# A linear-attention and spectral-mixing kernel on one core: batch 0 loaded in pieces with square-root norms, late transposes moved to transfers, and a new order of the work

## Chip, cores and metric

The kernel runs on one core of one Trainium2 chip. The metric is the device time of one launch in microseconds (us). Inputs and output lie in the chip's memory (HBM) as float32. The engines of the core are TensorE (PE for its matmuls, PEld for its weight loads), VectorE (DVE), ScalarE (ACT), GpSimd (POOL) and SyncE (SP). SP computes nothing here; it issues transfers. POOL also issues transfers, above all those that turn float32 into float16 on the way.

## What is computed

```python
# q, k, v: (8 batches, 8 heads, 576 tokens, 64);  D = C = 512 = 8 * 64
kv  = einsum('bhsd,bhse->bhde', k, v)
raw = einsum('bhsd,bhde->bhse', q, kv)
x   = raw / sqrt(mean(raw**2, -1) + 1e-6) * g_norm      # then heads side by side: (8, 576, 512)

theta = x @ w_theta
zr, zi = x * cos(theta), x * sin(theta)
y   = einsum('ts,bsd->btd', w_tok_r, zr) + einsum('ts,bsd->btd', w_tok_i, zi)
u   = x + y
out = u + maximum(u @ w_ch, 0)
```

## The kernel before

The 576 tokens of a batch are cut into five tiles: four full ones of 128 tokens (j = 0 to 3) and a tail of 64 (j = 4), which is folded, two half-widths one above the other, so that it fills 128 partitions with 256 columns. The eight batches go through the same stages. For one batch b these are, by the names of the tasks that the order is written in:

- **load k, load v, load q**: k and v come in as float32 on SP's queue (those of batch 0 in halves of two head pairs each, k on SP's queue and v on ACT's). q comes in as float16 on POOL's queue, which also brings `wth` (w_theta) and the two token weights `toki` and `tokr`. `wch` (w_ch) comes in as float32 into the buffer of z of batch 1 and is scaled into float16 by four tasks `wc`. A tiny transfer `hold s` on SP reads the token weight `toki`; everything behind it on SP's queue waits until that has landed.
- **kv** (matmuls, L272 for batch 0, L279 else) and **ko** (copy into the block-diagonal `kbd`).
- **qt, qo**: q turned by TensorE against the identity and copied out, for batches 0 and 1. From batch 2 on (`QD = 2`) a transfer does it instead, **qd**: a DMA transpose issued by SP.
- **raw** (q times kv, L338 and L347), **sq** (square, ACT), **ss** (sum per head, DVE), **rt** (power of -1/2, POOL, L376), **x** (DVE, L399): the norm. Code for a norm by square root (ACT, **sr**) and reciprocal (DVE, **rc**) is there, but its condition `b < 0` is never met.
- **xt, xo**: x turned by TensorE, 4 turns of 128 columns for a full tile and 2 for the tail, then copied out of PSUM with the scale g into `xT`.
- **th** (theta, L435 and L438), **pt** (ACT, L451), **ar** and **ab** (DVE, L457 and L465), **si** and **co** (sine and cosine, ACT, L473 and L480), **z** (DVE, L493). The tail's z goes into a buffer `zf`; four transfers **zv** on POOL's queue move its quarters into `zt`, where the tail's cosine and sine parts stand one above the other.
- **y** (token mixing, L516): `yH b c part` is half H of the tokens (256 or 320 columns), channel block c, in three parts of three matmuls. Part 0 needs z of tiles 0 and 1, part 1 that of tile 2, part 2 that of tile 3 and `zt`. **wt, wo** turn the token weights for it at the start, in nine groups. **um** (DVE, L521) makes u.
- **ut, uo**: u turned back by TensorE and copied out on ACT. **v** (u times w_ch), **fin** (DVE, L556: maximum with 0 and the sum), **st** (store, SP).

The order is written out by hand: `TURNS` lists the numbers of all tasks, `play` issues them in that order, and each engine works its own instructions strictly in the order in which they were issued. A letter behind a number puts a copy on another engine (A for ACT, D for DVE). `r16` and `r4` are idle matmuls that keep TensorE running at the start. So a task that waits holds everything that stands behind it on its engine or queue, whatever that needs. Buffers limit how far ahead a stage can run: 4 accumulators in PSUM (`acc`), 2 for turned tiles (`tr`), 2 for raw, 2 buffers of k and v, 3 of z.

## Time and profile before

| What | Value |
|---|---|
| runs of the kernel before | 222.97, 224.63, 227.66 us; median 224.63 |
| profiled execution, its own time | 224.09 us |
| its span, first to last instruction | 222.3 us |
| mean granted TensorE clock | 0.977 |
| read from HBM, written to HBM | 33.06 MB, 9.44 MB |

The span is shorter than the profiled execution's time by 1.8 us. An instruction in the profile is named by its line in the kernel, its engine, and the tiles that it writes and reads. A matmul row "x4" is four matmuls. Matmuls overlap in the array, so the step from one to the next, which the chain of waits shows, is shorter than the duration of one.

### The profile page before, as it was taken

To read this page: it belongs to the slowest core of one execution; us is meant where nothing else is said; L and a number is where in the kernel's file an instruction comes from. 1 tells how busy PE (TensorE), PEld (TensorE's weight loads), DVE (VectorE), ACT (ScalarE), POOL (GpSimd) and SP (SyncE) were. 2 spreads that over 40 slices of the span, in tenths; PEclk is the share of its full clock that TensorE was granted. 3 is DMA by queue.
4 is the path that set the end of the run, shared out by engine and by line. 5 is a ranking of instruction groups with operands and counts; after the bars stand their busy time and mean duration, and the time that the engine had idled before them with its cause. 6 is when DMAs were issued, how large, how long until landed. Compare 5 with 4: busy or idle time off the path is not lost.

```text
span 222.3 us, 5652 instructions
## 1 busy us (share of the span) xinstructions
PE 202.9 (91%) x2266; PEld 143.2 (64%) x2266; DVE 175.2 (79%) x358; ACT 131.6 (59%) x258; POOL 103.4 (47%) x112
## 2 busy tenths in 40 slices
PE   7397896958999999899999999999999999999992
PEld 2295555634777776676685777776676766676760
DVE  4028677849898798978999899799989889978552
ACT  2036257534685369765999559778564978565041
POOL 8208601599448376536765439380926034212000
PEclk9969799987999999999999999999999999999999
DMA  6999999998969999958999999399734004204324
GB/s 213 243 210 195 252 256 363 282 216 97 169 115 136 232 359 300 202 131 232 289 167 198 218 346 167 93 266 227 209 98 146 0 12 133 86 21 128 111 69 170
DMA packets 58731, 40.88 MB, mean 184 GB/s; under 512 B 28114, under 2 KB 52306, under 8 KB 58706
## 3 DMA queue, kind: packets, MB, share of 16 engines
q1 hardware_dynamic: 43474, 31.73, 55.6%
q0 software_dynamic: 14688, 7.62, 25.1%
q10 hardware_dynamic: 544, 1.18, 1.6%
q8 instruction: 18, 0.29, 0.5%
q14 instruction: 7, 0.06, 0.1%
HBM read 33.06 MB, written 9.44 MB: 191 GB/s over the span
## 4 chain that ended last, share of the span: by engine, by line
PE 64%; DMA 24%; POOL 4%; issue 2%; SPq 2%; DVE 2%; ACT 0%; POOLq 0%; DVEq 0%
PE y L516 30%; DMA vt<-in_v_dram 11%; PE v L435 9%; PE th L435 9%; DMA wn<-in_moe_w_tok_i_dram 7%; PE kv L279 5%; PE xps L296 3%; PE ups L296 3%; PE raw L338 2%; DMA zt<-zf 2%; DMA qe<-in_q_dram 2%; DMA out_dram<-ot 2%; PE th L438 2%; POOL rt L376 2%; SPq L194 1%
## 5 line engine op out<-in xcount | busy, mean ns | idle before, releaser
L376 POOL TENSOR_TENSOR rt<-ss,mhalf 128x8 f32<-128x8 f32 (+1 forms) x40 | 62.1, 1556 | 60.2 <-DVE ss L369 56.7
L516 PE MATMUL y<-wT,zm 128*128 128x320 f16 (+1 forms) x512 | 77.9, 287 | 0.7 <-DVE zm L493 0.7
L516 PEld LDWEIGHTS <-zm 128*128 128x128 f16 x512 | 47.8, 98 | 15.2 <-DVE zm L493 0.9
L521 DVE SCALAR_TENSOR_TENSOR wn<-y,gcol,xT 128x320 f16<-128x320 f32 (+1 forms) x64 | 32.0, 511 | 8.9 <-PE y L516 8.6
L435 PE MATMUL th<-wth,xT 128*128 128x512 f16 x128 | 33.6, 390 | 0.0
L451 ACT ACTIVATE pt<-th 128x512 f32<-128x512 f32 (+1 forms) x40 | 22.0, 553 | 17.5 <-PE th L435 16.2
L435 PE MATMUL v<-wch,wn 128*128 128x512 f16 x128 | 32.1, 379 | 0.0
L499 POOL DMA_DIRECT2D zt<-zf x32 | 17.6, 557 | 30.5 <-DVE zf L493 17.0
L480 ACT ACTIVATE sc<-arg,quarter 128x512 f16<-128x512 f32 (+1 forms) x40 | 26.8, 675 | 3.8 <-DVE arg L465 3.8
L542 ACT ACTIVATE us<-ups 128x512 f32<-128x512 f16 (+1 forms) x40 | 21.6, 551 | 12.3 <-PE ups L296 11.0
L556 DVE SCALAR_TENSOR_TENSOR ot<-v,us 128x512 f32<-128x512 f32 (+1 forms) x40 | 25.0, 632 | 4.3 <-ACT us L542 1.8
L457 DVE SCALAR_TENSOR_TENSOR arg<-pt,th 128x512 f32<-128x512 f32 (+1 forms) x40 | 24.8, 628 | 2.2 <-ACT pt L451 1.7
L473 ACT ACTIVATE sc<-arg 128x512 f16<-128x512 f32 (+1 forms) x40 | 23.1, 586 | 5.1 <-DVE arg L457 5.1
L369 DVE TENSOR_REDUCE ss<-sqb 128x8 f32<-128x520 f32 x32 | 22.0, 687 | 4.2 <-ACT sqb L360 4.1
L360 ACT ACTIVATE sqb<-raw 128x512 f32<-128x512 f32 x32 | 19.0, 595 | 10.0 <-PE raw L338 9.6
L399 DVE TENSOR_TENSOR x<-raw,rt 128x512 f16<-128x512 f32 x32 | 21.9, 684 | 3.7 <-POOL rt L376 3.7
L493 DVE TENSOR_TENSOR zm<-x,sc 128x1024 f16<-128x1024 f16 x32 | 21.7, 685 | 2.1 <-ACT sc L480 1.9
L279 PE MATMUL kv<-vt,kt 128*64 128x64 f32 x560 | 18.6, 223 | 3.1 <-DMA vt<-in_v_dram 3.1
L251 ACT ACTIVATE xT<-xps,gcol 128x512 f16<-128x512 f16 (+1 forms) x24 | 15.1, 632 | 10.1 <-PE xps L296 10.0
L279 PEld LDWEIGHTS kv<-vt,kt 128*64 128x64 f32 x560 | 17.5, 138 | 4.3 <-issue 1.9
L516 PE MATMUL y<-wT,zt 128*128 128x320 f16 (+1 forms) x64 | 18.8, 294 | 0.6 <-DMA zt<-zf 0.6
L435 PEld LDWEIGHTS <-xT 128*128 128x128 f16 x128 | 12.0, 101 | 10.2 <-issue 1.4
(73 smaller groups left out, 237.1 us busy)
## 6 DMA issues: line engine op xcount, KB each, us to landing
out_dram<-ot SPq DMA_DIRECT2D x32, 256.0 KB, 3.0
kt<-in_k_dram SPq DMA_DIRECT2D x7, 1024.0 KB, 7.5
vt<-in_v_dram SPq DMA_DIRECT2D x7, 1024.0 KB, 10.9
qh<-in_q_dram POOLq DMA_DIRECT2D x7, 512.0 KB, 10.2
kt<-in_k_dram SPq DMA_DIRECT2D x2, 576.0 KB, 4.8
vt<-in_v_dram ACTq DMA_DIRECT2D x2, 576.0 KB, 9.4
zm<-in_moe_w_ch_dram SPq DMA_DIRECT2D x1, 1024.0 KB, 11.5
zt<-zf POOLq DMA_DIRECT2D x32, 32.0 KB, 3.6
```

Source lines behind the costliest of these rows:

```text
L279: nc.tensor.matmul(t[i * D:(i + 1) * D, hp - lo, :], kt[b % NKV][:, 2 * hp + i, j, :], vt[b % NKV][:, 2 * hp + i, j, :], start=(j == 0), s ...
L369: nc.vector.reduce_sum(out=ss[:], in_=sq_sb.pop((b, j))[:], axis=AXX)
L376: nc.gpsimd.tensor_tensor(out=rt[:], in0=ss[:], in1=mhalf[:, 0:h], op=ALU.pow)
L399: nc.vector.tensor_tensor(out=x_pair[b, p][:, :, a * HC:(a + 1) * HC].rearrange("p t (h e) -> p h t e", e=D), in0=r[:].rearrange("p (h t e ...
L435: nc.tensor.matmul(t[:], lhs[:, kc, columns(j)], w[:, kc, :], start=first, stop=last)
L451: nc.scalar.activation(out=pt[:], in_=th_ps[b, j][:], func=AFT.Copy, bias=MAGIC)
L457: nc.vector.scalar_tensor_tensor(out=arg[:, 0, :], in0=pt_sb.pop((b, j))[:], scalar=MAGIC, in1=th_ps.pop((b, j))[:], op0=ALU.subtract, op1 ...
L473: nc.scalar.activation(out=sc[:, 0, :], in_=arg_sb[b, j][:, 0, :], func=AFT.Sin, bias=0.0, scale=-TURN * SHRINK,)
L480: nc.scalar.activation(out=sc_sb[b, j][:, 1, :], in_=arg_sb.pop((b, j))[:, 1, :], func=AFT.Sin, bias=quarter[:], scale=-TURN * SHRINK,)
L516: nc.tensor.matmul(t[:, 0:hi - lo], s, wT[:, w, lo:hi], start=n == 0, stop=n == len(z) - 1)
L521: nc.vector.scalar_tensor_tensor(out=uTb[b % NUT][:, c, lo:hi], in0=y_ps.pop((b, h, c))[:, 0:hi - lo], scalar=gcol[:, 0:1], in1=xTb[b % NX ...
L556: nc.vector.scalar_tensor_tensor(out=ot[:], in0=v_ps.pop((b, j))[:], scalar=0.0, in1=u_sb.pop((b, j))[:], op0=ALU.max, op1=ALU.add,)
```

## The change

- **Loads of batch 0.** k and v come in three pieces (head pairs 0 and 1, pair 2, pair 3), k and v in turn, all on SP's queue. `hold s` now reads the first piece of v instead of the token weight. Behind it stand, in this order, `wch`, k and v of batch 1, and k and v of batch 2; before, `wch` stood behind batch 1. On POOL's queue the token weight `toki` now stands ahead of `wth`, and q of batch 1 follows the token weights directly. All four `wc` go to POOL.
- **Norms of batch 0** by square root on ACT and reciprocal on DVE, instead of the power on POOL. The table of the square root is loaded at the start, that of the sine after the last square root (task `sn`).
- **Tail of z in batches 0 and 1** (`ZD = 2`): four multiplications on DVE write the quarters straight into `zt`, instead of one multiplication into `zf` and four transfers.
- **x of batches 5, 6 and 7** (`XD = 5`) is turned by DMA transposes on SP (tasks `xd`), two full tiles in one, the tail by itself. `xo` then reads SBUF instead of PSUM.
- **u of batches 5 and 6**, full tiles (`UD`), is turned by DMA transposes on SP (tasks `ud`, two buffers). For these `um` writes u in another layout, with one more instruction for the half that holds the tail; ACT takes the maximum with 0 out of PSUM (task `vo`), and `fin` adds the turned u to it.
- **fin** writes over one of its inputs; the buffers `us` and `ot` (three each) become one ring of five.
- **TURNS** is new throughout. The parts of it that matter are quoted by the names of the tasks in the prediction.

```diff
@@ play order: all of TURNS is replaced
@@ numbers
     QD = 2
+    XD = 5
+    UD = (5, 6)
+    ZD = 2
...
+    NUD = 2
+    NOT = 5
@@ x turned by transfers
+    def x_turn_dma(b, p):
+        if p < 2:
+            d = work.tile([P, 2 * NKC, P], FP16, tag="qD", bufs=4, name="xd")
+            src = x_pair[b, p][:].rearrange("p t c -> p (t c)")
+            tr_ps["x", b, 2 * p], tr_ps["x", b, 2 * p + 1] = d[:, 0:NKC, :], d[:, NKC:2 * NKC, :]
+        else:
+            d = work.tile([P, NKC // 2, P], FP16, tag="qTe", bufs=3, name="xd")
+            src, tr_ps["x", b, NJ] = x_sb[b, NJ], d[:]
+        nc.sync.dma_start_transpose(out=d[:], in_=src)
@@ z_make
+        if not full(j) and b < ZD:
+            for i in range(2):
+                for hh in range(2):
+                    at, to = slice(hh * TL, (hh + 1) * TL), slice((1 - i) * TL, (2 - i) * TL)
+                    nc.vector.tensor_tensor(
+                        out=zt[b % NZ][to, hh * HC:(hh + 1) * HC],
+                        in0=x[at, :], in1=sc[at, i, :], op=ALU.mult,
+                    )
+            return
@@ u_make
+        parts = [(uTb[b % NUT][:, c, lo:hi], lo, hi)]
+        if b in UD:
+            parts = [(u_units(b)[:, 2 * h:2 * h + 2, c * P:(c + 1) * P], lo, lo + 2 * P)]
+            if h:
+                parts.append((u_at(b, c, NJ), SM, S))
...
+    def u_turn_dma(b, j):
+        d = work.tile([P, NKC, P], FP16, tag="ud", bufs=NUD, name="ud")
+        nc.sync.dma_start_transpose(out=d[:], in_=u_units(b)[:, j, :])
+        u_sb[b, j] = d[:].rearrange("p n c -> p (n c)")
+
+    def positive(b, j):
+        d = work.tile([P, C], FP32, tag="us", bufs=NOT, name="vs")
+        nc.scalar.activation(out=d[:], in_=v_ps.pop((b, j))[:], func=AFT.Relu)
+        v_ps[b, j] = d
@@ finish
+        if full(j) and b in UD:
+            ot = v_ps.pop((b, j))
+            nc.vector.scalar_tensor_tensor(
+                out=ot[:], in0=u_sb.pop((b, j)), scalar=TURN, in1=ot[:], op0=ALU.mult, op1=ALU.add,
+            )
+        else:
+            ot = u_sb.pop((b, j))
...
@@ loads of batch 0
-    for a, (lo, hi) in enumerate(((0, NH2), (NH2, NHP))):
-        both = [add(f"load {x}0{'ab'[a]}", e, lambda e=eng, t=t, src=src, lo=lo, hi=hi: pairs_in(e, t[0], src, 0, lo, hi))
-                for x, e, eng, t, src in (("k", "SP", nc.sync, kt, k), ("v", "ACT", nc.scalar, vt, v))]
+    for a, (lo, hi) in enumerate(((0, NH2), (NH2, NH2 + 1), (NH2 + 1, NHP))):
+        both = [add(f"load {x}0{'abc'[a]}", "SP",
+                    lambda t=t, src=src, lo=lo, hi=hi: pairs_in(nc.sync, t[0], src, 0, lo, hi))
+                for x, t, src in (("k", kt, k), ("v", vt, v))]
...
-    add("hold s", "SP", lambda: hold_sync(wn[1][0:1, 0, 0:1]), got["tok", 0])
+    add("hold s", "SP", lambda: hold_sync(vt[0][0:1, 0, 0, 0:1]), [early])
@@ norms of batch 0
-            if b < 0:
+            if b == 0:
                 sr = add(f"sr {b} {j}", "ACT", lambda b=b, j=j: square_root(b, j), [ss])
                 rt = add(f"rc {b} {j}", "DVE", lambda b=b, j=j: reciprocal(b, j), [sr], [("rt" + w, 4)])
@@ start
-        table(AFT.Sin)
+        table(AFT.Sqrt)
```

More of the change, by code (lines that the diff above doesn't have):

```diff
@@ L173 @@
     gate = const.tile([1, 1], FP32, name="gate")
-    gate_s = const.tile([1, 1], FP16, name="gate_s")
+    gate_s = const.tile([1, 1], FP32, name="gate_s")
     def full(j):
@@ L434, in dense @@
             if full(j):
-                nc.tensor.matmul(t[:], lhs[:, kc, columns(j)], w[:, kc, :], start=first, stop=last)
+                nc.tensor.matmul(t[:], lhs(kc), w[:, kc, :], start=first, stop=last)
             else:
@@ L520, in u_make @@
         lo, hi = HALVES[h]
[L521 to L524 removed]
+        y = y_ps.pop((b, h, c))
+        parts = [(uTb[b % NUT][:, c, lo:hi], lo, hi)]
[3 more added lines that the diff above has]
+                parts.append((u_at(b, c, NJ), SM, S))
+        for dst, s0, s1 in parts:
+            y_in, x_in = y[:, s0 - lo:s1 - lo], xTb[b % NXT][:, c, s0:s1]
+            if s1 - s0 == 2 * P and b in UD:
+                y_in, x_in = (a.rearrange("p (j s) -> p j s", j=2) for a in (y_in, x_in))
+            nc.vector.scalar_tensor_tensor(
+                out=dst, in0=y_in, scalar=gcol[:, 0:1], in1=x_in, op0=ALU.mult, op1=ALU.add,
+            )
     def u_turn(b, j):
[L527 removed]
         if full(j):
[L529 removed]
+            turned("ups", lambda i: u_at(b, i, j), NKC, ("u", b, j))
             return
@@ L540, in u_out @@
         n, e = (NKC, "") if full(j) else (NKC // 2, "e")
-        d = work.tile([P, n * P], FP32, tag="us" + e, bufs=3, name="us")
+        d = work.tile([P, n * P], FP32, tag="us" + e, bufs=NOT, name="us")
         nc.scalar.activation(
```

141 lines of the change are left out of this document (88 added, 53 removed), and 42 rows, old and new, of the table TURNS.

## Prediction

> **What bounds the kernel now.** I read the page first, then the stretches before and after the point where batch 0's token mixing is done, then the chain of waits.
>
> ```profile
> span 222.3 us, 5652 instructions
> ...
> PE 202.9 (91%) x2266; PEld 143.2 (64%) x2266; DVE 175.2 (79%) x358; ACT 131.6 (59%) x258; POOL 103.4 (47%) x112
> ...
> PE   7397896958999999899999999999999999999992
> ...
> DVE  4028677849898798978999899799989889978552
> ...
> PEclk9969799987999999999999999999999999999999
> DMA  6999999998969999958999999399734004204324
> ```
> TensorE (PE) is busy nearly throughout from the eleventh slice on (a slice is 5.6 us), VectorE (DVE) is close behind it; in the first ten both have gaps, while the transfers run at nine tenths.
>
> ```profile
> 0.00:60.00 60.00, 46.54 (x523) 31.92 (x524) 36.97 (x86) 25.67 (x49) 32.14 (x41) 0.91 1.06 228
> 60.00:217.30 157.30, 155.71 (x1742) 111.21 (x1741) 137.15 (x272) 105.56 (x210) 71.29 (x71) 1.00 0.75 167
> ```
> The columns are busy time and, in brackets, instructions. Busy time of PE is modelled, so I count its work from steps in the chain of waits (start, length, what):
>
> ```profile
> 57.48 0.22 PE xps L296 x4
> ...
> 58.66 0.86 PE th L435 x4
> 59.52 0.33 PE y L516 x3
> ...
> 61.05 0.56 PE th L438 x8
> ...
> 61.61 2.33 PE kv L279 x80
> ...
> 101.18 0.25 PE raw L347 x8
> ...
> 143.56 0.41 PE y L516 x3
> ```
> One batch: y 4 x 3 x (0.33 + 0.41) = 8.9 us; theta 4 x 0.86 + 0.56 = 4.0, and the same for v; the turns of x and of u, 18 x 0.055 each, 2.0 together; kv 2.3; raw, four tiles like a turned tile and the tail, 1.1. That is 22.3, or 178.4 for eight. Batch 0's kv has 144 instructions instead of 80, 1.9 more; turning the token weights (45 turns) adds 2.5 and q of batches 0 and 1 adds 2.0: 185 us of work in a span of 222.3, so 37 are lost. The last part of batch 0's mixing starts at 59.52. By 59.9 PE has done 30.6: batch 0 without v and u (19.2), the 2.5 and 2.0, and of batch 1 kv, raw, four turned tiles and three thetas (6.9). So **29 of the 37 us are lost in the first 60**.
>
> ```profile
> 216.92 1.03 PE L435 MATMUL v<-wch,wn 128*128 128x512 f16 x4
> ...
> 218.30 0.69 DVE L556 SCALAR_TENSOR_TENSOR ot<-v,us 128x512 f32<-128x512 f32 x1 [0.65 <-DMA out_dram<-ot]
> ```
> The last four matmuls start at 216.92, done at 217.8. From 59.9 to there 154.3 us of work take 158, so the middle loses 3.6, and 4.5 follow behind the last matmul. Lost: head 29.3, middle 3.6, end 4.5.
>
> **The head, what it waits for now.**
>
> ```profile
> 5.09 15.70 DMA wn<-in_moe_w_tok_i_dram
> ...
> 46.81 4.10 DMA qe<-in_q_dram
> ```
> ```profile
> 10.05 3.11 PE L272 MATMUL kv<-vt,kt 64*64 64x64 f32 x72 [3.53 <-DMA vt<-in_v_dram]
> ...
> 13.10 1.04 PE L296 MATMUL qps<-ident,qh 128*128 128x128 f16 x8
> ...
> 15.54 0.62 PE L338 MATMUL raw<-kbd,qT 128*128 128x128 f16 x8
> ...
> 17.45 4.89 POOL L376 TENSOR_TENSOR rt<-ss,mhalf 128x8 f32<-128x8 f32 x3 [3.69 <-DVE ss L369]
> ...
> 20.81 0.72 SPq L238 DMA_DIRECT2D gate_s<-wn  x1
> ...
> 25.34 0.68 DVE L399 TENSOR_TENSOR x<-raw,rt 128x512 f16<-128x512 f32 x1
> ```
> ```profile
> 47.42 0.68 DVE L493 TENSOR_TENSOR zm<-x,sc 128x1024 f16<-128x1024 f16 x1
> ```
> Batch 0's first kv waits for v until 10.05, the turned q starts at 13.10, the norms pass one by one through POOL from 17.45, the last x of a full tile ends at 26.0, and z of tile 3 at 48.1. SP issues nothing behind `hold s` until toki is there (20.81). The 4.10 are a stall: PE stands at `qte 1 4` for q's tail of batch 1, issued too late.
>
> **The change in the head.** The prices on ACT and DVE, and the transfers:
>
> ```profile
> L480 ACT ACTIVATE sc<-arg,quarter 128x512 f16<-128x512 f32 x32 | 22.8, 717 | 3.1 <-DVE arg L465 3.1
> L369 DVE TENSOR_REDUCE ss<-sqb 128x8 f32<-128x520 f32 x32 | 22.0, 687 | 4.2 <-ACT sqb L360 4.1
> L399 DVE TENSOR_TENSOR x<-raw,rt 128x512 f16<-128x512 f32 x32 | 21.9, 684 | 3.7 <-POOL rt L376 3.7
> ...
> L473 ACT ACTIVATE sc<-arg 128x512 f16<-128x512 f32 x32 | 19.8, 629 | 2.8 <-DVE arg L457 2.7
> ...
> L451 ACT ACTIVATE pt<-th 128x512 f32<-128x512 f32 x32 | 19.0, 596 | 16.2 <-PE th L435 16.2
> ...
> L251 ACT ACTIVATE xT<-xps,gcol 128x512 f16<-128x512 f16 x18 | 12.2, 686 | 5.8 <-PE xps L296 5.7
> ...
> L301 ACT COPY wT<-wps 128x576 f16<-128x576 f16 x3 | 1.9, 633 | 4.9 <-PE wps L583 4.9
> ...
> L390 ACT ACT_TABLE_LOAD x1 | 1.3, 1283 | 0.7 <-PEq L806 0.7
> ```
> ```profile
> kt<-in_k_dram SPq DMA_DIRECT2D x2, 576.0 KB, 4.8
> ...
> zm<-in_moe_w_ch_dram SPq DMA_DIRECT2D x1, 1024.0 KB, 11.5
> zt<-zf POOLq DMA_DIRECT2D x32, 32.0 KB, 3.6
> ...
> wn<-in_moe_w_tok_r_dram POOLq DMA_DIRECT2D x1, 576.0 KB, 17.7
> ...
> qD<-qh SPq DMA_TRANSPOSE x12, 5.2
> ```
> Loads: the first pieces of k and v are as large as the two halves of k now (4.8 us each from issue, one close behind the other), so kv can start near 6.5 instead of 10.05. But `qt 0 0` is second on PE's queue and q lands as before, near 13.1; behind it stand kv 0 1, `qt 0 2` and kv 0 2, 36 instructions a pair at 0.035 to 0.043 (3.11 / 72), so the first raw comes at 16, no earlier than now: the early kv is hidden by q.
>
> Norms: from `ss 0 2` at 16.8 to `x 0 3` DVE has 18 instructions, four ss (2.7), four x (2.7), five tiny ones and five of about 0.45: 8 us, so x ends at 25 instead of 26, and tiles 0 and 1 by 22.7. The power on POOL (three in 4.89) is gone; ACT gets five roots and a table load (1.28) ahead of `pt 0 1`. That load is hidden, since theta needs xo and its turn first; uncovered it costs 1.3. The Trainium skill ("ScalarE: Activation LUTs", What ACT_TABLE_LOAD costs) gives a switch of tables about 2.66 us with its drain; by that, my sum would be at most 1.4 later. The row here has one load at an idle start and can't show a drain.
>
> From theta at 24 ACT has four full tiles of pt, si, co (4 x 1.94 = 7.8), the tail's three (about two thirds, 1.3), four `wo` (2.5) and two xo (1.4): 13.0, so the last cosine ends at 37 and z of tile 3 at 37.7, if nothing else is late. The token weight tokr can be: `wt 1` now stands ahead of `th 0 3` on PE. Tokr lands at 23.9 now (issued 6.16, 17.7), after POOL's stream had the engines to itself. In the new order `hold s` opens at 6.5 to 10, and behind it wch, k and v of batch 1 come at once. Between 13.1 and 23.9 POOL's stream needs 11 us alone; at half the engines it needs 22 and tokr comes at 35. From tokr to z of tile 3 there are theta, pt, three `wo`, two si, the tail's cosine, two co and z: 8 us. So z ends between 37.7 and 43; I take 38.7, nearer to the first, since 35 needs the other queue to take half of the engines all the way.
>
> Then PE has left, up to the last part `y0 0 2 2`: y 8.9 less the four first parts and two second ones that can run before (2.4), q of batch 1 0.9, one turned u 0.2, kv 1 2.3, two raws 0.4: 10.3. It ends at 49, with 26.6 us of work done (19.2, 0.2, 2.5, 2.0, 2.3, 0.4). Lost 22.4 instead of 29.3: **-6.9** (bounds -7.9 and -2.6). The written-in-place z takes four POOL transfers (3.6 us to land) out of each of two batches, and adds three small DVE multiplications; tile 3's z is later, so it gives nothing here. q's tail of batch 1 is issued behind two `wc`, which wait for wch on POOL; q of batch 2 stands behind them too. It is needed near 47. Wch takes 11.5 now and 23 at half the engines, from 10 to 33 at worst, then two `wc` and the 4.10: it fits, and if it doesn't PE stands as it does now.
>
> **Behind the head.** (a) **Valley.** The old order has batch 1's theta in hand at 60; the new one starts batch 1's norms only then. DVE has 24 instructions from `ss 1 0` to `z 1 1`, at 0.504 each (137.15 / 272) 12.1, behind a square; PE has v 0, turned tiles, theta 1 and kv 2, 12.7. z of tiles 2 and 3 needs 12 more on DVE, 6; PE has eight parts of y and two raws, 3.9. I take **+2** (0 to 6).
> (b) **Turns off PE.** x of three batches 54, u of two 32: 86 x 0.055 = **-4.7** (0 if PE then waits for DVE).
> (c) **DVE.** Its queue holds 304 instructions behind that point, against 272 behind the old one: 304 x 0.504 = 153 us. PE needs 185 - 4.7 - 26.6 = 153.7. DVE ran at 137.15 / 157.3 = 87% there; now both must run near 95%. The page shows slices with both at 9, so I take **+2** (0 to 16, see the first rival).
> (d) **Late transfers.** A turned x took 0.22 on PE; as a transfer it takes 5.2 to land like q's, behind what SP has queued. For batches 5 and 6 some 20 us of PE work lie between x and its theta. For batch 7 `xd 7 2` stands on SP behind `ud 5 2`, whose buffer is free only after `fin 5 0`; from `raw 7 3` to `th 7 3` PE has 12 us (y 6, two thetas, tails), and the chain square, sum, power (1.6), x, 5.2 and xo takes about 11 with an issue. **+1** (-1 to 6). Behind those issues stand stores, with five output buffers instead of three. `vo` takes the place of `uo` on ACT. No row shows xo and fin reading SBUF instead of PSUM; I take the same durations, and a fifth of them either way, for 12 xo and 8 fin some 2.5 us, counts only where DVE or ACT paces.
> (e) **End.** A half tile is stored last, and the last fin no longer waits 0.65 for a store: **-1** (-1.5 to 0).
>
> Sum: -6.9 + 2 - 4.7 + 2 + 1 - 1 = -7.6. The profiled execution took 224.1 (span 222.3 and 1.8 around it), so 216.5; the median of the runs is 0.5 above it: **217 us**.
>
> **Rivals.**
> *VectorE becomes the bound (slower).* Place: DVE's queue behind 49, above all the eight `fin` of batches 5 and 6 that wait for turned u, with everything behind them. At the old share of 87%, 153 us take 176: span 49 + 176 + 3.5, time 230.8 with the median. It passes 2% slower below a share of 88%, and it is my forecast at 94%. For it: DVE's count grows while PE's work falls, and the transfers (5.2) stand in a two-buffer ring. Against: transfers leave SP's queue mostly empty after 160, where the page's DMA row shows 4 and less. The Trainium skill speaks against the change here: "VectorE: DVE Perf Modes", The three transpose paths, has 390 ns on TensorE and 1309 ns by DMA for a 128x128 turn, and the rules below it prefer TensorE. By those, each turned tile is later, as in (d), and this rival the likelier. The trace agrees in direction: 0.22 for four turns on PE, 5.2 for a transfer. Chance 0.15, from the rows alone.
> *All covered.* No valley, no tightness, no late transfer, z at 37.7: 217 - 6 = 211. For it: the old middle lost 3.6 in 158, so an order can hide such waits. 0.24.
> *Weights crowded out.* z at 43: 217 + 4.5 = 221.5. For it: the DMA row is at 9 there, with no room beside it. Against: it needs the hardware queue to keep half until 35, and SP has issued what batch 1 needs before that. 0.17.
> *The change doesn't do what it says.* If squares and copies between the roots needed tables of their own, some eight loads of 1.28 would come back into the head: 10 us, 227. Only one load stands in the old page for squares, copies and sines, which speaks against. 0.04.
> *Forecast* 0.40, own range 212.5 to 221.
>
> 2% of 224.6 is 4.5, about what a measurement of this kernel can tell from no change: 220.1 and 229.1. Faster: 0.35 of the forecast, 0.24, and 0.05 of the crowded case, 0.64. Slower: the first rival and 0.02 of the rest, 0.17. Within: 0.19. The range 209 to 228 leaves out the bottom of the covered case (0.05) and most of the first rival (0.13).
>
> **What would show it.** `y0 0 2 2` done near 49 (before: 59.9), x of batch 0 by 25, z of tile 3 at 38 to 40; a DVE share of 94% from there; turned u landing before its fin asks for it; `th 7 3` without a wait over 1 us; one output store after the last matmul. I am wrong if tokr lands after 35, or if PE idles for more than 10 us between 49 and the end with DVE named as the releaser.

## The result, and the profile after

The changed kernel took 221.55 us (median of 18 runs, 219.56 to 222.68), the kernel before 225.78 beside it (18 runs). The ratio is 0.9863, with an interval of 0.9827 to 0.9899: 1.4% faster (3.1 us), where 3.4% were forecast and 217.0 us. The ratio leaves out executions more than 1.5% above the fastest of the same kernel, which is why it is nearer to 1 than the quotient of the two medians; the profiles of runs 1 and 11 below are of such longer executions, so their spans are not compared. The profiled execution of the changed kernel has a span of 220.9 us, against 222.3. It took 222.68 us, the longest of the 18 runs and 1.1 us above their median, while the profiled one of the kernel before (224.09) lies a little below the middle of its runs; so the two traces differ by 1.4 us only, and the account below is of those 1.4 us.

The page of the changed kernel, the same lines as before (busy time and share by engine, then tenths in slices of 5.5 us):

```profile
span 220.9 us, 5506 instructions
...
PE 200.5 (91%) x2177; PEld 137.7 (62%) x2177; DVE 175.2 (79%) x371; ACT 132.2 (60%) x268; POOL 97.3 (44%) x102
...
PE   7398699799799999989999999999999999999991
...
DVE  4018649627989989897999988999997999999662
...
PEclk9969769999999999999999999999999999999998
DMA  6999999954999999959999976998980776764374
```

PE has 89 matmuls fewer, 86 of them the turns; in the last quarter the DMA row is at 0 to 7, mostly at 6 or 7, where it had 0 to 4. The two stretches of the prediction, by busy time and instructions:

```profile
0.00:60.00 60.00, 47.45 (x525) 31.97 (x525) 32.57 (x77) 28.01 (x60) 24.23 (x33) 0.91 1.01 221
60.00:217.30 157.30, 153.07 (x1656) 105.76 (x1653) 142.61 (x295) 104.18 (x208) 73.02 (x70) 1.00 0.88 190
```

VectorE did 4.4 us less in the first 60 us (32.57 against 36.97) and 5.5 more behind them: 142.61 of 157.3, 91%.

Busy time of PE is modelled, so both traces were counted as the prediction did it: each matmul at the step at which matmuls of its kind follow each other (0.055 us for a turn, 0.11 and 0.137 for the two kinds of y, 0.215 for 512 columns), summed by the time at which it starts; the matmuls that only fill time were left out. That is 184.4 us of work in the kernel before and 179.6 in the changed one. What the clock shows beyond the work done so far is lost. The table gives the time lost up to a moment, in us, for the two kernels and for four that are told of below:

| up to | 20 | 30 | 40 | 50 | 60 | 80 | 120 | 210 | end |
|---|---|---|---|---|---|---|---|---|---|
| before | 14.0 | 19.1 | 23.0 | 27.5 | 29.3 | 30.1 | 32.0 | 33.6 | 37.9 |
| changed | 13.7 | 20.4 | 24.7 | 25.5 | 28.3 | 31.4 | 35.0 | 36.3 | 41.3 |
| changed, once more | 13.7 | 20.3 | 24.3 | 25.0 | 27.7 | 30.8 | 34.3 | 35.7 | 40.8 |
| hold alone (e1_hold_token) | 13.7 | 17.9 | 23.0 | 24.6 | 27.1 | 30.0 | 33.4 | 34.8 | 39.8 |
| order alone (o1_order) | 13.8 | 20.8 | 24.3 | 26.1 | 26.5 | 29.1 | 33.0 | 34.4 | 39.0 |
| both (b1_hold_order) | 14.0 | 18.4 | 20.9 | 23.3 | 24.1 | 26.6 | 30.1 | 31.8 | 36.5 |

Batch 0's mixing was done at 59.9 us in the kernel before, with 29.3 lost; in the changed one it is done at 52.8. I end the head at 50, with 25.5 lost; the 0.9 lost from 50 to 52 are waits for copies of batch 1's kv. So the head gained 3.8 us (2.9, if it is ended at the last part of the mixing, as the prediction did). From there to 80 us 5.9 more are lost; from 80 to 210 it is 4.9, where the kernel before lost 4.3 from 60 on (+0.6); behind 210 it is 5.0 against 4.3 (+0.7). With 4.8 us of work less: -3.8 + 5.9 - 4.8 + 0.6 + 0.7 = -1.4, the difference of the spans.

**The head.** The first kv, q's first turn and the last parts of `y0 0 2 2`, from the timeline of PE (start, length, line, operation, tiles, shapes, count, idle time before and its releaser), and the last x of a full tile on DVE:

```profile
6.21 1.26 PE L278 MATMUL kv<-vt,kt 64*64 64x64 f32 x36
11.55 0.61 PE L302 MATMUL qps<-ident,qh 128*128 128x128 f16 x4 [4.07 <-DMA qh<-in_q_dram]
...
52.65 0.27 PE L554 MATMUL y<-wT,zt 128*128 128x256 f16 x1
```
```profile
24.01 0.69 DVE L405 TENSOR_TENSOR x<-raw,rt 128x512 f16<-128x512 f32 x1
```

Kv starts at 6.2 instead of 10.05, PE then waits for q, and x is done at 24.7: as forecast (q itself came at 11.55, 1.5 us earlier than assumed). Then the chain of waits, the granted clock, and the transfer of the theta weight in the kernel before:

```profile
5.42 20.46 DMA wth<-in_moe_w_theta_dram
...
25.92 1.86 PE th L464 x4
...
40.60 0.70 DVE zm L531
```
```profile
24.00:32.00 8.00, 5.93 (x31) 2.97 (x31) 3.83 (x9) 4.04 (x8) 5.20 (x6) 0.57 1.19 224
```
```profile
wth<-in_moe_w_theta_dram POOLq DMA_DIRECT2D x1, 512.0 KB, 12.9
```

The theta weight, issued at 5.42, lands at 25.9, and the first theta waits for it, not for x. In the kernel before it took 12.9 us from issue to landing, and was there at 17.3. The first theta then takes 1.86 us for four matmuls that take 0.86 to 1.04 elsewhere: the granted clock is 0.57 in these 8 us (the column ahead of the DMA share; 0.79 in the kernel before). z of tile 3 is done at 41.3, not at 38.7.

**Behind the head.** The chain of waits from 51 to 74 us:

```profile
51.80 0.36 PE raw L344 x3
...
52.81 0.71 DVE ss L375
...
53.66 0.90 POOL rt L382
...
55.31 1.64 POOL rt L382
56.95 0.93 POOL qh L212
57.88 0.65 POOL qe L218
58.53 3.50 POOL rt L382 x2
62.05 0.69 DVE x L405
...
72.80 0.70 DVE zm L531
...
73.55 4.42 PE y L554 x36
```

Batch 1's first raw starts at 51.3. Behind it POOL has four powers and, between the second and the third, two requests for q of batch 3: 8.4 us up to 62.0. From there to the last z the chain runs along DVE nearly without a break, and part 2 of batch 1's y starts at 73.55. PE does other work meanwhile, but 5.9 us of it are gaps.

**The turns and the late batches.** The rows of the new transfers in the view of transfers (count, median us from issue to landing), and all that PE waited for from 80 us to the end, by the view of waits (us in total, times, longest):

```profile
xd<-x SPq DMA_TRANSPOSE x9, 3.2
ud<-wn SPq DMA_TRANSPOSE x8, 2.5
```
```profile
PE xps L302 <- DVE x L405: 1.1, 1, 1.1
PE raw L344 <- DVE x L405: 0.3, 1, 0.3
```

Both end by 101.2 us. From 120 us to the end the view has no row at all for PE.

### The profile page after: what moved, and what is told of

It reads as the page before. It is cut to its first block, busy times and chain, and to the rows that moved or that the text cites. A ratio compares the mean times of both kernels' runs of the same rounds, so it can differ in the third digit from the quotient of the medians.

```text
span 220.9 us, 5506 instructions
## 1 busy us (share of the span) xinstructions
PE 200.5 (91%) x2177; PEld 137.7 (62%) x2177; DVE 175.2 (79%) x371; ACT 132.2 (60%) x268; POOL 97.3 (44%) x102
## 4 chain that ended last, share of the span: by engine, by line
PE 60%; DVE 14%; DMA 9%; POOL 8%; ACT 5%; issue 2%; POOLq 0%; DVEq 0%; ACTq 0%
PE y L554 26%; PE v L464 10%; PE th L464 10%; DMA wth<-in_moe_w_theta_dram 9%; POOL rt L382 5%; PE kv L285 5%; DVE arg L486 2%; DVE ss L375 2%; PE ups L302 2%; PE raw L344 2%; DVE x L405 2%; DVE zm L531 2%; PE th L467 2%; PE xps L302 1%; PE v L467 1%
## 5 line engine op out<-in xcount | busy, mean ns | idle before, releaser
L382 POOL TENSOR_TENSOR rt<-ss,mhalf 128x8 f32<-128x8 f32 (+1 forms) x35 | 54.9, 1572 | 81.7 <-DVE ss L375 81.5
L554 PE MATMUL y<-wT,zm 128*128 128x256 f16 (+1 forms) x512 | 76.0, 286 | 1.9 <-DVE zm L531 1.0
L569 DVE SCALAR_TENSOR_TENSOR wn<-y,gcol,xT 128x256 f16<-128x256 f32 (+2 forms) x72 | 32.6, 478 | 8.2 <-PE y L554 7.7
L464 PE MATMUL th<-wth,xT 128*128 128x512 f16 x128 | 34.2, 395 | 2.0 <-DMA wth<-in_moe_w_theta_dram 1.6
L464 PE MATMUL v<-wch,wn 128*128 128x512 f16 x128 | 31.6, 379 | 0.0
L366 ACT ACTIVATE sqb<-raw 128x512 f32<-128x512 f32 x32 | 18.5, 592 | 14.7 <-PE raw L344 13.4
L617 DVE SCALAR_TENSOR_TENSOR us<-v,us 128x512 f32<-128x512 f32 (+1 forms) x32 | 19.4, 616 | 2.0 <-PE v L467 0.8
L307 ACT CAST kbd<-kv 64x256 f16<-64x256 f32 (+1 forms) x28 | 9.4, 334 | 19.1 <-PE kv L278 12.4
L464 PEld LDWEIGHTS <-xT 128*128 128x128 f16 x128 | 11.6, 100 | 13.4 <-issue 3.3
L588 ACT ACTIVATE us<-ups 128x512 f32<-128x512 f16 (+1 forms) x32 | 17.0, 541 | 4.1 <-PE ups L302 2.6
L537 POOL DMA_DIRECT2D zt<-zf x24 | 13.6, 574 | 12.4 <-PE v L467 11.1
L464 PEld LDWEIGHTS <-wn 128*128 128x128 f16 x128 | 11.8, 98 | 11.2 <-issue 0.6
```

Source lines behind the costliest of these rows:

```text
L382: nc.gpsimd.tensor_tensor(out=rt[:], in0=ss[:], in1=mhalf[:, 0:h], op=ALU.pow)
L464: nc.tensor.matmul(t[:], lhs(kc), w[:, kc, :], start=first, stop=last)
L554: nc.tensor.matmul(t[:, 0:hi - lo], s, wT[:, w, lo:hi], start=n == 0, stop=n == len(z) - 1)
L569: nc.vector.scalar_tensor_tensor(out=dst, in0=y_in, scalar=gcol[:, 0:1], in1=x_in, op0=ALU.mult, op1=ALU.add,)
```

## Experiments

Times are medians; a ratio is that to the kernel before, run beside it on the same chip, with its 95% interval. The times of one kernel spread by 1 to 2%, so differences below 1 us are read from the traces as well.

**1. Who crowds the head: SyncE's hold.**

```diff
-    add("hold s", "SP", lambda: hold_sync(vt[0][0:1, 0, 0, 0:1]), [early])
+    add("hold s", "SP", lambda: hold_sync(wn[1][0:1, 0, 0:1]), got["tok", 0])
```
`hold s` stands behind `load tokie` in the order, and the tiny buffer that it reads into is float16 again; nothing else is changed.

> One part undone: SyncE's hold waits again for the first token weight (toki) and not for the first two pairs of v of batch 0, so the channel weight and k and v of batch 1 are asked for later. Theory (the early release crowds GpSimd's weights and eats part of the head's gain): wth lands by about 20 us (25.9 in the changed kernel, 17.3 in the kernel before), tokr by about 25 (28.8), the theta of tile 1 starts near 24.2 instead of 25.9, z of tile 3 of batch 0 is done by about 40 (41.3), and the time is 1 to 2 us shorter than the changed kernel's (so 2.0 to 3.0% below the kernel before), as long as the later v of batch 1 is there before its kv (47.5). Rival (the same bytes through the same queues, one late load is swapped for another): wth lands earlier, but kv of batch 1 or the channel weight comes later by as much, and the time stays within 0.5 us of the changed kernel's.

220.26 us, ratio 0.9853 (0.9800 to 0.9905). The transfer of the theta weight, the first theta, and three windows with the granted clock:

```profile
wth<-in_moe_w_theta_dram POOLq DMA_DIRECT2D x1, 512.0 KB, 14.3
...
24.07 1.03 PE L464 MATMUL th<-wth,xT 128*128 128x512 f16 x4
```
```profile
24.00:32.00 8.00, 7.55 (x63) 4.38 (x61) 7.30 (x14) 7.94 (x16) 5.06 (x5) 1.00 1.21 274
32.00:40.00 8.00, 5.20 (x38) 3.68 (x38) 6.65 (x13) 4.39 (x8) 4.97 (x6) 0.91 1.27 257
40.00:50.00 10.00, 9.84 (x139) 7.97 (x138) 2.98 (x6) 2.24 (x5) 0.00 (x0) 0.91 0.88 198
```

The weight lands at 19.7 instead of 25.9. Theta no longer waits, and it runs at full clock: by 30 us 17.9 are lost instead of 20.4, and z of tile 3 is done at 38.3 instead of 41.3. But batch 1's raw starts only 1.3 us earlier (50.05 against 51.34): PE has no gap in batch 0's y in either run, and in this one the stretch at half clock came later and fell into that y, so that the granted clock is 0.91 from 32 to 50 where the changed kernel has 1.00. The ratio moved by no more than its error. The theory of the crowding holds for the place; as a gain by itself it is not shown.

**2. Pulling batch 1 ahead, first try.** Only turns are moved: `kv 1`, its copies, `qt`, `raw`, `sq`, `ss`, `rt` and `x 1 0`, `x 1 1` go into batch 0's y.

> Only the written order is changed: batch 1's kv, its copies, q turns, raw products, squares, sums, roots and first x are pulled ahead into batch 0's token mixing. Theory (the loss of 5.9 us between 50 and 80 us is a valley of waits: batch 1's chain over ScalarE, VectorE and GpSimd starts only when TensorE has run out of batch 0's work): raw of batch 1 starts near 43 instead of 51.3, y of batch 1 part 2 near 68 instead of 73.6, the loss between 50 and 80 us falls from 5.9 to about 2 us, the time is 3 to 4 us shorter than the changed kernel's. Rival (VectorE sets the pace from 50 us on, so an earlier start of batch 1 only moves the same VectorE work): the loss between 50 and 80 moves behind 80 us, and the time stays within 1 us of the changed kernel's.

222.32 us, 0.9962 (0.9922 to 1.0002): no gain, though batch 1's raw starts at 43.6, as the theory had it; part 2 of its y still starts at 73.0. The first row of the view of waits shows where it went:

```profile
PE raw L344 <- DVE qT L309: 2.3, 1, 2.3
```

In this order DVE stood for POOL's powers ahead of `x 1 0` and `x 1 1` (1.26 and 0.93 us, up to 48.9), with two results of batch 0 and the copy of q behind them that PE needed. The loss from 50 to 80 us is 5.3 instead of 5.9. So the run does not speak for the rival (VectorE's pace), nor for an early start as enough; the order was a bad one, and what it was meant to test stayed open until run 9.

**3. The roots of batch 0.**

```diff
+        return                     # square_root: no step on ScalarE
...
-        nc.vector.reciprocal(out=rt[:], in_=sq_sb.pop((b, j))[:])
+        nc.gpsimd.tensor_tensor(out=rt[:], in0=sq_sb.pop((b, j))[:], in1=mhalf[:, 0:h], op=ALU.pow)
```

> One part undone: batch 0's norms go by GpSimd's power again (1.65 us for one in the trace) instead of ScalarE's square root and VectorE's reciprocal; the two table loads in the middle go too. Theory (the theta of tile 1 waits for wth at 25.9 anyway, and the x of batch 0 end at 24.7, so of what the roots save only about 1 us counts): the x of batch 0 end 2 to 4 us later, near 27 to 28, and the time is 0.5 to 2 us longer than the changed kernel's. Rival (the whole latency of the roots stands on the path of the head, and GpSimd's weight issues and powers get in each other's way): 3 to 4 us longer. Other rival (the norms are hidden altogether): within 0.4 us.

222.58 us, 0.9987 (0.9940 to 1.0034). The last x of a full tile is done at 28.5 (27.79 + 0.69), 3.8 us later; theta starts 0.95 us later (26.87 against 25.92). At 50 us 26.6 are lost, 1.1 more than in the changed kernel, at 80 us 0.7 more. By the ratios the roots are worth 1.2%, by the traces 0.8 us: most of the 3.8 us is hidden behind wth.

**4. The turns, back on PE.** `XD = 8` and `UD = ()`, and each `xt` and `ut` just ahead of the place of its copy.

> One part undone: x of batches 5 to 7 and u of batches 5 and 6 are turned by TensorE again, at about the places where the copies of the turned tiles stood. Theory (from 80 us to the end TensorE is the one that has no room; its work falls from 184.4 to 179.6 us by these turns): the time is 3 to 5 us longer than the changed kernel's, about that of the kernel before or a little above. Rival (VectorE paces the later batches, TensorE has idle time there): within 1 us, with TensorE's idle time in the last batches smaller by the 4.7 us of the turns.

231.07 us, 1.0385 (1.0303 to 1.0466): 9.5 us longer, of which the matmuls are 4.8. The chain shows the rest as waits that the new places made: a copy of u waits for an output buffer, this for a store, and PE for the copy.

```profile
185.22 2.32 DMA out_dram<-us
187.56 0.39 ACT us L589
188.00 0.40 PE ups L303 x4
```

A second version has one more output buffer (`NOT = 6`) and copies and stores nearer to the turns:

> Once more x of batches 5 to 7 and u of batches 5 and 6 turned by TensorE, with the places mended where the first version made TensorE wait for copies and stores of its own (one more buffer for the finished tiles, the copies and stores nearer to their turns). Theory (TensorE has no room there, so the turns cost what they take): the loss between 160 and 200 us is under 1.5 us and the time 4 to 6 us longer than the changed kernel's. Rival (the transfers did more than take TensorE's work away: with the turns on TensorE the copies behind them hold up VectorE and ScalarE too): again 8 us or more. Other rival (the turns hide in idle time): under 2 us.

230.65 us, 1.0234 (1.0173 to 1.0294), with 3.9 us lost from 160 to 200: 9.1 us longer, the rival's 8 or more. Then each turn by itself:

> Only x of batches 5 to 7 is turned by TensorE again (54 matmuls, 3.0 us of TensorE's time); u of batches 5 and 6 stays with the transfers. Both together cost 9 us where their matmuls take 4.8. Theory (TensorE has no room in the late batches, each undo costs its matmuls, and the rest of the 9 us is the places that the turns of u were given): 2.5 to 4 us longer than the changed kernel's. Rival (it is the turns of x, whose copies ScalarE and VectorE wait for, that cost the rest too): 6 us or more.

> Only u of batches 5 and 6 is turned by TensorE again (32 matmuls, 1.8 us), its copies at the places where ScalarE took the relu of the product before, with one more buffer for finished tiles. Theory (the places of these turns, each just ahead of its copy, cost more than their matmuls): 4 to 7 us longer than the changed kernel's, with 2 us or more lost between 170 and 200 us beside the changed kernel. Rival (a turn costs its matmuls and nothing else, so the surplus stands with x): 1.5 to 2.5 us longer.

x alone: 228.71 us, 1.0163 (1.0107 to 1.0219). u alone: 225.89 us, 1.0013 (0.9974 to 1.0051). Against the changed kernel that is 7.2 and 4.4 us for 3.0 and 1.8 us of matmuls, so the surplus stands with both. In both the trace has waits behind 120 us, where the changed kernel has none; the longest of each:

```profile
176.49 0.38 PE L303 MATMUL xps<-ident,x 128*128 128x128 f16 x4 [1.27 <-DVE xT L260]
```
```profile
189.33 0.71 PE L554 MATMUL y<-wT,zm 128*128 128x256 f16 x5 [0.83 <-DVE us L617]
```

No undo came cheaper than its matmuls, as it would if PE had room there. How much of the surplus is the turns' own price, and how much the places that they were given, is not settled: in the kernel before, which was ordered with turns on PE, only 1.6 us are lost from 120 to 210.

**5. Is it VectorE's capacity?** The changed kernel once more, and then two kernels that move work from DVE to ACT without touching batch 1's chain.

> The changed kernel itself once more, beside the runs that follow, so that they are compared with it on the same chip and not over two sittings. Expected: 0.986 of the kernel before, as measured, within 0.004; a loss curve within 1 us of the first one everywhere.

221.52 us, 0.9858 (0.9817 to 0.9899).

```diff
+        elif b == 0:
+            ot = u_sb.pop((b, j))
+            nc.scalar.activation(out=ot[:], in_=v_ps.pop((b, j))[:], func=AFT.Relu)
```

In the second run the condition is gone: it is every batch, without the full tiles of batches 5 and 6, which end in another way.

> The five last steps of batch 0 go from VectorE to ScalarE as a plain relu of the channel product; the addition of u is left out for that batch. VectorE is spared five operations of 0.68 us (3 us with the tail), four of them before 75 us; nothing of batch 1's chain is touched. Theory (VectorE's capacity sets the pace from 58 us until batch 1's last z): the loss between 50 and 80 us falls from 5.9 by 1.5 to 2.7 us, y of batch 1 part 2 starts near 71.5 instead of 73.6, and the time is 1.5 to 2.5 us shorter than the changed kernel's. Rival (a valley of waits: raw, square, sum, 1.65 us powers, x, turn, theta, sine one behind the other): the loss there and the time stay within 0.6 us.

221.45 us, 0.9859 (0.9807 to 0.9911): no difference. The stretch from 50 to 80 us, first the changed kernel, then this one:

```profile
50.00:80.00 30.00, 26.81 (x300) 18.11 (x299) 27.05 (x55) 18.62 (x39) 15.17 (x12) 1.00 0.97 195
```
```profile
50.00:80.00 30.00, 26.53 (x296) 17.75 (x295) 24.87 (x51) 20.23 (x43) 15.18 (x12) 1.00 0.91 196
```

DVE has 2.2 us less to do (27.05 to 24.87), and PE loses 6.2 instead of 5.9.

> The same for every batch but 5 and 6, whose full tiles finish in another way: 32 operations (about 20 us) leave VectorE, whose busy time falls from 175 to about 155 us, and ScalarE takes them as plain relus (132 to about 150 us); the addition of u is left out there. Theory (VectorE paces the whole middle, with 92% of the time busy): beside the valley's 1.5 to 2.7 us the 4.6 us that are lost between 80 and 200 us fall to under 1.5, and the time is 4 to 6 us shorter than the changed kernel's. Rival (TensorE paces the middle behind the valley; VectorE's 92% are what is left beside it): the loss between 80 and 200 us stays at 3.5 us or more and the time gains no more than in the run with batch 0 alone, within 1 us.

224.28 us, 0.9983 (0.9948 to 1.0018): 16 us off DVE (175.2 to 159.2), and the kernel is 2.8 us slower than the changed one, which neither the theory nor the rival had. From 80 us on PE now waits 3.3 us by the view of waits, where the changed kernel has 1.4; the largest row, with ScalarE gone from 132.2 to 145.6 us:

```profile
PE th L464 <- ACT xT L257: 0.9, 2, 0.6
```

VectorE is 91% busy behind 60 us, and yet work moved from it to ScalarE gives nothing back, so it does not pace by itself. What its relief would give if ScalarE did not take 13.4 us in exchange, these runs do not show.

**6. Is it POOL's row of powers?** `load q3` and `load q3e0` are moved behind `rt 1 3`; then batch 1's powers become reciprocals on DVE; then all of them.

> One order changed: GpSimd asks for q of batch 3 (two issues, 1.6 us in the trace) behind the four full powers of batch 1 and not between the second and the third. VectorE's capacity fell as a cause in the run with batch 0's last steps on ScalarE: five operations fewer changed nothing. New theory (the valley is GpSimd's row of four powers of 1.65 us and those two issues, 8.4 us from 53.4 to 61.7, behind which x, theta and z of batch 1's second pair stand): x of tile 3 comes 1.6 us earlier (60.4), y of batch 1 part 2 starts near 72.2 instead of 73.6, the loss between 50 and 80 us falls by 1 to 1.5 us, and the time by as much. Rival (the second half of the valley, where VectorE goes from one operation straight into the next from 61 to 73.5 us, takes the gain back): within 0.5 us.

221.75 us, 0.9917 (0.9885 to 0.9948). y of batch 1 part 2 starts at 73.3 instead of 73.6: the rival. POOL's timeline shows why the two requests were nearly free:

```profile
58.29 3.24 POOL L382 TENSOR_TENSOR rt<-ss,mhalf 128x8 f32<-128x8 f32 x2 [1.40 <-DVE ss L375]
```

Without them the third power waits 1.40 us for its sum on DVE, and the four are done at 61.5 instead of 62.0.

```diff
+        if b == 1:
+            nc.vector.reciprocal(out=rt[:], in_=ss[:])
```

> Batch 1's norms are a reciprocal on VectorE (0.12 us) instead of GpSimd's power (1.65 us); the square root is left out for that batch. Theory (the row of powers makes the valley): the x of batch 1's second pair come about 5 us earlier (near 57), the loss between 50 and 80 us falls from 5.9 to 2 us or less, y of batch 1 part 2 starts at 69 to 70, and the time is 3 to 4 us shorter than the changed kernel's. Rival (raw of batch 1 comes too late, at 51.3, and from there theta, sine and z take what they take): the loss falls by 1.5 us at most.

220.89 us, 0.9848 (0.9792 to 0.9904). The chain without a single power in it:

```profile
52.70 0.69 DVE ss L375
...
53.79 0.11 DVE rt L383
...
72.01 0.70 DVE zm L534
...
72.76 4.42 PE y L557 x36
```

Part 2 starts at 72.8, 0.8 us earlier, and the loss from 50 to 80 us is 5.2. The theory fell: POOL's row of 8.4 us stood in the chain, but without it the chain is nearly as long.

> The same in all batches from 1 to 7: no power on GpSimd at all, the square root left out everywhere but in batch 0. Theory (only in batch 1 does the row of powers stand on the path; later batches have their norms long before they are needed): the same time as with batch 1 alone, within 0.7 us, and 3.5 to 4.6 us still lost between 80 and 200 us. Rival (the powers hold up later batches too, 81.9 to 103 us above all): another 1 to 3 us shorter, with the loss between 80 and 120 us falling from 3.6 to under 2 us.

221.31 us, 0.9871 (0.9820 to 0.9923): as with batch 1 alone.

**7. Both at once.** The edits of e6 and e9 together:

> Both halves of the valley's second part are lightened at once: the last steps of batch 0 on ScalarE (the addition of u left out) and the roots of batch 1 as reciprocals on VectorE (the square root left out). Alone, the first changed nothing and the second gained 0.6 us. Theory (two rows of equal length, GpSimd's powers to 61.7 us and VectorE's unbroken row from 55 to 72.8 us, so that each hides the gain of the other): y of batch 1 part 2 starts near 71 instead of 73.6, the loss between 50 and 80 us is 3.5 to 4.2 us instead of 5.2 and 6.2 with the one or the other, and the time 1.5 to 2.5 us shorter than the changed kernel's. Rival (neither row counts, batch 1's kv and raw start too late, near 51.3, and the chain behind them is long): the loss stays at 5 us or more, the time within 1 us of the changed kernel's.

221.09 us, 0.9786 (0.9747 to 0.9825); beside it, on the same chip, e12_end, which is the changed kernel with another tail, took 221.16: by the medians the gain of 1.5 to 2.5 us did not come. In the trace part 2 starts at 70.85, and from 50 to 80 us 4.6 are lost (28.7 - 24.1). There the edits together do more than the sum of each (5.2 and 6.2 alone), so that two rows of work lay beside each other; but 4.6 remain with neither the powers nor DVE's extra work. The larger part must lie in when the chain begins and in what stands ahead of it on each engine.

**8. The end.** `ute 7 4`, `ve 7 4` and its stores ahead of `v 7 1`, `st 7 10` last.

> Only the last twenty turns are put in another order: the tail of batch 7 is worked off ahead of the last full tile, so that a full tile of 256 KB is stored last, as in the kernel before, and not two halves of 64 KB. In the changed kernel 4.3 us pass from VectorE's last result to the end of the span, in the kernel before 3.3. Theory (the two small stores stand in line behind a full one, with SyncE's issues one behind the other): about 3.3 us from VectorE's last result, the time 0.5 to 1 us shorter. Rival (the last store waits for the stores ahead of it whatever its size): within 0.3 us.

221.16 us, 0.9793 (0.9746 to 0.9840). From DVE's last result (216.1) to the end of the span it is 3.6 us instead of 4.3, but DVE's last step now waits 0.73 for PE, and behind 210 us 4.9 are lost, as in the changed kernel (5.0). No gain. The order of the last stores is not what cost the end 0.7.

**9. The valley by the order alone.** The turns from 38 to 90 us in a new order, with nothing left out: `kv 1` in pieces between parts of batch 0's y, then raw, squares, sums and powers; three copies of q on ScalarE; no x on DVE ahead of work that is ready; q of batch 3 behind the powers.

> Nothing left out: only the written order between 38 and about 90 us is changed, better than in the first try at it. Batch 1's kv stands in the middle of batch 0's token mixing, its raw, squares, sums and powers follow at once, the copies of its q go to ScalarE, no x stands on VectorE ahead of work whose input is there already, and q of batch 3 is asked for behind the powers. Theory (batch 1's chain starts too late, and its powers stand in a row): powers from about 47 us instead of 53.4, y of batch 1 part 2 near 69 to 70 instead of 73.6, the loss between 50 and 80 us 2 to 3 us, and the time 2.5 to 4 us shorter than the changed kernel's (217.5 to 219 against 221.5). Rival (as in the first try, each wait that is removed comes back at another place, because k and v of batch 1 land at 38.8 us only): within 1 us of the changed kernel's.

220.36 us, 0.9814 (0.9764 to 0.9863). Raw of batch 1 starts at 49.0, the first power at 51.2, part 2 at 71.67. From 50 to 80 us 3.0 are lost instead of 5.9, but 0.6 more before 50, and by the medians 1.2 us are gained, less than the 2.5 to 4 of the theory. Theta still waited for wth, up to 26.8 in this run, and kv of batch 1, whose inputs land near 39, came to its turn on PE at 43.1.

**10. Order and hold together.** The order of run 9 and the hold of run 1:

> Nothing left out: the new order between 38 and 90 us, which cut the loss of the valley from 5.9 to 3.0 us, together with SyncE's hold waiting for the first token weight again. Theory (the two losses are separate, one in the head and one behind it): the theta of tile 1 near 24.2 us, the loss at 50 us 24 to 25 (26.1 with the order alone), at 80 us 27 to 28 (29.1), the time 1 to 1.5 us below the one with the order alone, 218.5 to 219.5. Rival (k and v of batch 1 land a little later through the hold, and the new order needs them at 40 us): TensorE waits for them near 40 us and the time is the same as with the order alone, or longer.

217.10 us, 0.9620 (0.9577 to 0.9664), 4 us below e11 and e12 on the same chip and below the 218.5 to 219.5 of the theory. Its window from 24 to 32 us, PE's longest wait from 38 to 80 us, and the first row of batch 1's powers, which start at 48.35 instead of 53.66:

```profile
24.00:32.00 8.00, 7.29 (x60) 4.31 (x60) 6.59 (x16) 7.92 (x15) 4.03 (x6) 1.00 1.19 292
```
```profile
PE kv L285 <- DMA vt<-in_v_dram: 0.7, 1, 0.7
```
```profile
48.35 3.29 POOL L382 TENSOR_TENSOR rt<-ss,mhalf 128x8 f32<-128x8 f32 x2 [10.45 <-DVE ss L375]
```

Now z of tile 3 of batch 0 is ready at 38.0, and PE starts batch 1's kv at 39.4, between parts of the y that this z frees; it waits 0.7 us for the last of v. At 50 us 23.3 are lost, at 80 us 26.6; part 2 of batch 1's y starts at 68.8. Each alone gave little, and the timelines suggest why: with the hold alone batch 1's kv still stood behind most of batch 0's y, at 46.2; with the order alone batch 1's kv stood behind a y that came late. Some of the 4 us are the clock: its mean over the six runs is 0.991, over those of e12 0.981. In the 18 runs of the changed kernel a hundredth of clock goes with 1.1 us (a line fitted to them), so by estimate it is 1 us of the 4.

**11. More of the same behind 90 us.**

> As the last one, with the order of the last turns changed as above and the turns between 90 and 210 us moved a little too (x and theta of the next batch some places earlier). Theory (3.6 us are lost between 80 and 120 us by waits of the same kind, for x of batch 2 near 95 us): a further 1 to 2.5 us, 216.5 to 218.5. Rival (behind 90 us the engines run as they must, and another order only moves the waits): within 0.7 us of the last one, on either side.

221.71 us, 0.9807 (0.9758 to 0.9856): 4.6 us worse than run 10, at the same mean clock (0.991). The largest wait behind 80 us in its trace is 2.0 us that run 10 does not have:

```profile
PE y L554 <- DMA zt<-zf: 2.0, 1, 2.0
```

How much of the 4.6 us this wait makes up is not shown.

## Why the prediction was wrong

*The sign and the turns were right.* 86 turns less are 4.8 us of PE's work by the count (4.7 forecast), and nothing took their place: from 120 us on PE waits for nothing. The Trainium skill's preference for TensorE ("VectorE: DVE Perf Modes", The three transpose paths and the rules below it) made the first rival the likelier. The trace agrees with its direction, 2.5 and 3.2 us for a transfer of a tile or pair against 0.22 for four turns, but here the time lay beside other work.

*The step that failed is the valley, term (a).* It took +2 between its bounds of 0 and 6, from DVE's 12.1 us and PE's 12.7 side by side. They do lie so, but behind a start that the step itself had put at 49 and that came at 51.3, and DVE's work is not free to begin there: square, sum, four powers with two requests between them, x, turn, theta, sine and z follow one another. PE had other work for 24 of the 30 us. It measured 5.9, the upper bound. Nor is it one row: DVE's relief alone took nothing from it, the powers alone 0.7, both 1.3, the order of run 9, which starts the chain 2.3 us earlier and puts no waiting x ahead of work that is ready, 2.9. An earlier start in a poor order (run 2, 7.7 us earlier) gave 0.6. How the 5.9 divide between the start and the places is open.

*The head, -6.9, was mis-sized: -3.8.* The mechanism was right up to x at 24.7. The sum then watched tokr (it landed before 29, well within the 24 to 35) and gave no row to wth, which travels on the same queue, now behind toki, and came at 25.9 where it had come at 17.3. With the hold restored it came at 19.7 (run 1), so 6.2 of the 8.6 us are the early release; its new place behind toki was not tried alone. The theta waited, and ran at a clock of 0.57; the two together are 2.6 us at z of tile 3 (41.3 for 38.7), and how they divide is open. The rest is the last stretch up to `y0 0 2 2`, 11.5 us for the 10.3 of the sum, of which 0.9 are counted behind the head here. The rival "weights crowded out" named the mechanism, the early release of `hold s`, and its 221.5 is the measured time (the bounds of its own sum, -6.9 and -2.6, give 4.3 and 221.3); but its place was tokr, and the larger miss lay in the valley, so that the agreement is luck.

*VectorE's tightness and the late transfers, +2 and +1, were 0.6 together.* The share went to 91%, close to the 94% forecast, without pacing by itself, and turned tiles landed in 3.2 and 2.5 us instead of 5.2. A kernel with 16 us of DVE's load moved to ScalarE was no faster. The two terms were 2.4 too high where the valley was 3.9 too low: together the three were forecast at +5 and measured 6.5, so part of the error in (a) was cancelled by luck. And 217.1 us, the forecast's time, came only in run 10, by another release, another order and a higher clock.

*The end, -1, was +0.7.* Storing a half tile last did not shorten it: two small stores stand behind a full one, and run 8 shows that the other order costs the same.

*The table load, at nothing, held.* It started at 23.67 and took 1.28, and ScalarE's next step began at 24.97, with theta not before 25.9. The 2.66 us that the Trainium skill gives for a switch ("ScalarE: Activation LUTs", What ACT_TABLE_LOAD costs) do not show: from the end of the last root (23.65) to the next step it is 1.3.

## What to carry to other kernels

When an earlier stage is made faster, ask what the next stage still has to wait for, and when its own chain can start: this head gave 3.8 us, and 5.9 were lost behind it, where the next batch's chain was put after it and not beside it. Two waits in a row can hide each other's price: undone alone they gave 1.3 us or less here, together 4, though some of that is a higher clock. A share of 91% is no proof that an engine paces by itself: take work off it, and look whether anything moves.

## What the runs showed of the hardware

The granted clock of TensorE falls to one half for some 3 to 10 us at a time in the first 52, and not at the same place in each execution of one program: between 25 and 32 us in one run of the changed kernel, between 20 and 31 in another. The second run with all turns back on PE (e46) has the same head; there the theta of tile 1 also started at 26.0, but took 1.02 us and not 1.86, and at 50 us 24.1 were lost instead of 25.0 to 25.5. Over the 18 runs of the changed kernel the time goes with the mean clock, if loosely: 222.68 us at 0.973 and 219.56 at 0.992. The three kernels with the hold restored have mean clocks of 0.987 to 0.991 over their runs, all the other variants and the changed kernel 0.975 to 0.981; so by the line of run 10, an estimate, about 1.0 of the 1.3 us that run 1 is below the changed kernel can be the clock. The Trainium skill ("TensorE: Matmul & The Clock Gate", What's actually happening) has a monitor with a freely running window that lowers the clock when the array was idle; the runs agree in so far as the stretch moves, and as with the hold restored, where PE does not stand before theta, the clock from 24 to 32 us is 1.00 (it is 0.91 from 32 to 50 in run 1, and 1.00 there in run 10). In e46 it is 1.00 from 24 to 32 as well, with theta as late as in the changed kernel. That the idle time causes it was not tried by itself.

SyncE's own queue was held in a way for which the view of waits names no releaser. Of the eight loads of k and v that follow the channel weight, all but the first (0.50 us) held it for 2.6 to 7.1 us before the next was issued. Why is not shown. The longest and the shortest:

```profile
8.98 7.05 SPq L206 DMA_DIRECT2D kt<-in_k_dram  x1
...
34.68 2.62 SPq L200 DMA_DIRECT2D vt<-in_v_dram  x1
```
